# A dense layer's norm: from per-token sums and diagonal matrices to column-strip sums and transfers, its steps begun earlier

## The chip, the core and the metric

The kernel runs on one core of a Trainium2 chip. What is measured is the device time of one execution, in microseconds (us). The core has five engines that run side by side, each taking its own instructions in the order in which the program issued them: TensorE (PE, with its weight loads PEld), VectorE (DVE), ScalarE (ACT), GpSimd (POOL) and SyncE (SP), which issues the DMA transfers. Engines wait for each other through semaphores only.

## What is computed

Three layers, one after the other, on 2 x 768 = 1536 tokens of width 512. Layer 1 is attention with 8 heads of 64, masked to keys whose 6-bit hash bucket is that of the query. Layer 2 is a dense gated layer that begins with a root-mean-square norm of each token, and layer 3 sends each token to one of 8 experts. The change touches the norm of layer 2 alone:

```
def _moe_ref(x, w_gate, w_val, w_out, rms_g):
    rms = np.sqrt(np.mean(x * x, axis=-1, keepdims=True) + 1e-06)
    xn = x / rms * rms_g
    g = xn @ w_gate
    silu = g * (1.0 / (1.0 + np.exp(-g)))
    val = xn @ w_val
    return (silu * val @ w_out).astype(np.float32)
```

## The kernel before

Activations lie transposed: features on the 128 partitions (four chunks of 128, `NK`), tokens along the free dimension, in three blocks of 512 tokens (`xyt[0]` to `xyt[2]`). A norm needs, for every token, a sum over features, which means over partitions and chunks, and then the root's inverse on every partition again. `xnorm(b)` returns the steps of that for block `b`:

- `square` (twice, on ACT): squares of two chunks each, 128x1024, into `xf`.
- `add` (three times, on DVE): the four squared chunks are added to one.
- `mean`: on PE, four products whose loaded weights are the 128 columns of squares and whose moving operand is one column of ones. The sums come out one token per partition, in PSUM (128x4). DVE scales them into `r`, POOL raises them to the power -1/2.
- `spill`, `flat`, `diag` (eight times), all on POOL: the 128x4 roots are split into a high and a low part, a tile of ones is written, and eight 128x128 diagonal matrices are made of the parts.
- `spread`: on PE, two products (128x512) of the tile of ones with the diagonals, so that every partition holds every token's root; ACT copies that to `rb`.
- `scale`, `high`, `low` (four times each): the normed chunks and their high and low parts in `RG`, which PE reads.

The order of the work is written out by hand. In `attention()` every step is put into a list with a position, `at(pos, step)`, and the list is issued in the order of the positions. One unit of attention (128 queries of one head) has 1000 positions, and there are 96 units. The unit's steps are `qk` (scores into one of two PSUM halves, L530 and L532), `stats` (DVE, row maximum, L545 and L546), `expo` (ACT, L559; the half is free again after it), `scales` (POOL, L554), `back` (PE transposes, L568, into one of three banks that `psH()` hands out in turn), `emptied` (copies of those, L572, on ACT or DVE) and, every four units, the product with the values (L589) and its copy (L599). The norm of block 0 stands at the positions of `PLAN["xn"]`.

In `moe1()` the dense layer runs in 36 steps `n`, 12 for each block. A step issues, in this order: the high and low parts of the weights of step n+1 (`split`, L317 on ACT, L318 on DVE or POOL), the gate and value products of step n (24 products of 128x512, L345 to L347) with their activation (ACT L750, DVE L751 and L752, ACT L754 for the high part `hh`), then what `win[n]` holds, with a PSUM half as argument, then what `cal[n]` holds, then `h_low(n)` (DVE L759) and the products `down(n-1)` (12 of 128x512, L770 to L772). Weights of the second half of this layer arrive as 64-bit floats and are converted on DVE and ACT in `cal[0]` to `cal[9]` (L244, L248, L252 and L792). The norms of blocks 1 and 2 are put into `win` and `cal` from step `o` on, which is step 0 for block 1 and step 13 for block 2:

```
            for f_ in win.pop(n, ()):
                f_(psA(True))
```

`psA(True)` is the PSUM half that the gate products of step n+1 write next. SP issues all transfers of this stretch: the rows of q, k and their hash bits to other partitions (L490, L493, L496, L514), loads (L238, L395, L403), and the result of a block (L778).

Of the kernel before, what the change touches and what calls it, by code (L numbers as in the profile page):

```python
# [15 lines left out]
P = 128  # L16
# [29 lines left out]
    "cv": (-4, 3532, 7612, 8983, 10967),  # L46
    "late": 2000,
    "v": 11280,
    "xn": ((59501, 60423), (62683, 62816, 63235), 64180, 61519, 64439, (71025, 67128, 68518, 70395), 72597, (74588, 92089, 73653, 83058), (86240, 93654, 83020, 84060), (89992, 93958, 86081, 95569)),
    "splits": ((-6894, 1, 0, 0), (-10825, 1, 0, 1), (-4899, 0, 0), (1381, 1, 1, 0), (8244, 1, 1, 1)),  # L50
    "ahead": ((215, 2), (3057, 4), (4742, 6), (17871, 8)),
    "batches": (2, 2, 3, 2, 3, 2, 3, 2, 3, 2),
# [27 lines left out]
def tile_kernel(  # L80
# [51 lines left out]
    def f32(ap):  # L132
        return ap.bitcast(F32)
# [16 lines left out]
    def rg(off, n, parts=P):  # L150
        return RG[0:parts, off : off + n]
# [108 lines left out]
    def xnorm(b):  # L260

        xf = ch4(BB[:, 0:2048])
        rb = EX[:, 1536:2048]
        at_ = X_AT[b] if b else 17 * S
        dg = [rg(at_ + y * 512, 512).rearrange("p (t q) -> p t q", t=TPB) for y in range(2)]
        st = {}

        def square(hf):
            sl = slice(2 * hf, 2 * hf + 2)
            nc.scalar.activation(out=xf[:, sl], in_=xyt[b][:, sl], func=AF.Square)  # L270

        def add(x):
            i, j = ((0, 2), (1, 3), (0, 1))[x]
            TT(out=xf[:, i], in0=xf[:, i], in1=xf[:, j], op=ALU.add)

        def mean(ps):
            for t in range(TPB):
                mm(ps[:, t : t + 1], lhsT=xf[:, 0, t * P : (t + 1) * P], rhs=ones[:, 0:1], start=True, stop=True)
            r = st["r"] = sp.tile([P, 2 * TPB], F32, tag="r", name="r", bufs=2)
            TS(r[:, 0:TPB], ps[:, 0:TPB], 1.0 / DM, 1e-6, ALU.mult, ALU.add)  # L280
            PTT(out=r[:, TPB:], in0=r[:, 0:TPB], in1=half, op=ALU.pow)

        def spill():
            r = st["r"]
            rr = st["rr"] = sp.tile([P, 2 * TPB], F32R, tag="rr", name="rr", bufs=2)
            copyP(out=rr[:, 0:TPB], in_=r[:, TPB:])
            PTT(out=rr[:, TPB:], in0=r[:, TPB:], in1=f32(rr[:, 0:TPB]), op=ALU.subtract)

        def flat():
            copyP(out=rg(at_ + 1024, P), in_=ones)  # L290

        def diag(z):
            PTS(dg[z // TPB][:, z % TPB], ident, f32(st["rr"][:, z : z + 1]), 1.0, ALU.mult, ALU.mult)

        def spread(ps):
            for y in range(2):
                mm(ps[:, 0:TB], lhsT=rg(at_ + 1024, P), rhs=dg[y].rearrange("p t q -> p (t q)"), start=(y == 0), stop=(y == 1))
            copyA(out=rb, in_=ps[:, 0:TB])

        def scale(k):  # L300
            STT(out=xf[:, k], in0=xyt[b][:, k], scalar=gcol[:, k : k + 1], in1=rb, op0=ALU.mult, op1=ALU.mult)

        def high(k):
            copyA(out=xpart(b, 0, k), in_=xf[:, k])

        def low(k):
            (PTT if b else TT)(out=xpart(b, 1, k), in0=xf[:, k], in1=f32(xpart(b, 0, k)), op=ALU.subtract)

        return dict(square=square, add=add, mean=mean, spill=spill, flat=flat, diag=diag, spread=spread, scale=scale, high=high, low=low)


    GV_AT = (4096, 10240)
# [366 lines left out]
    def attention():  # L679
        start_up()  # L680
        for u in range(NU):
            for name, f in (("qk", qk), ("exp", expo), ("tr", back), ("stats", stats)):
                at(PLAN["first"][name].get(u, 1000 * u + PLAN[name][u % 4]), f, u)
            for hf in range(2):
                at(PLAN["first"]["copy"].get(2 * u + hf, 1000 * u + PLAN["copy"][u % 4][hf]), emptied, u, hf)
        for u in range(0, NU, 2):
            at(PLAN["first"]["scales"].get(u, 1000 * u + PLAN["scales"][u // 2 % 2]), scales, u)
        for g in range(NU // 4):
            av_steps(g)
        for p in range(1, NPAIR):  # L690
            cast, low, q_rows, k_rows, ql_rows, bits, signs, place = prep(p)
            o = (p - 1) * PER * 1000 + (PLAN["late"] if p == 1 else 0)

            def put(name, f, *a):
                at(PLAN["first"]["pair"].get(name, o + PLAN[name]) if p == 1 else o + PLAN[name], f, *a)

            for j in range(2):
                put(f"cast{j}", cast, j)
                put(f"low{j}", low, j)
            put("q_rows", q_rows)  # L700
            put("k_rows", k_rows)
            put("ql_rows", ql_rows)
            put("bits", bits)
            put("signs", signs)
            put("place", place, 0)
            put("place2", place, 1)
            if p + 2 < NPAIR:
                put("load", load, p + 2)
            at((p - 1) * PER * 1000 + PLAN["v"], load_v, p)
        for x in range(12):  # L710
            for y, f in enumerate((cv_load, cv_rebias, cv_shift, cv_low, cv_sign)):
                at(max(6000 * x + PLAN["cv"][y], PLAN["ramp"]["cv"]), f, x)
        for x in range(12, 15):
            at(1000 * (NU - 9) + 500, cv_load, x)
        xn = xnorm(0)
        sq, ad, me, fl, sp_, dg, sd, sc, hi_, lo_ = PLAN["xn"]
        for x in range(2):
            at(sq[x], xn["square"], x)
        for x in range(3):
            at(ad[x], xn["add"], x)  # L720
        at(me, lambda: xn["mean"](psH()))
        at(fl, xn["flat"])
        at(sp_, xn["spill"])
        for z in range(2 * TPB):
            at(dg[z // 2], xn["diag"], z)
        at(sd, lambda: xn["spread"](psH()))
        for k in range(NK):
            at(sc[k], xn["scale"], k)
            at(hi_[k], xn["high"], k)
            at(lo_[k], xn["low"], k)  # L730
        for x_, f, *a in PLAN["splits"]:
            at(1000 * NU + x_, split_gv if f else split_o, *a)
        for x_, z in PLAN["ahead"]:
            at(1000 * NU + x_, gate_products, 0, 0, z)
        for _, _, f, a in sorted(cal, key=lambda z: z[:2]):
            f(*a)


    def moe1(rt):
# [57 lines left out]
        for b in range(1, NBLK):  # L797
            xn = xnorm(b)
            o = (b - 1) * NF + (0 if b == 1 else 1)
            cal[o].append(lambda f=xn["square"]: f(0))  # L800
            cal[o + 1].append(lambda f=xn["square"]: f(1))
            for x in range(3):
                cal[o + 2 + x].append(lambda f=xn["add"], x=x: f(x))
            win[o + 6].append(lambda ps, xn=xn: (xn["mean"](ps), xn["spill"](), xn["flat"](), [xn["diag"](z) for z in range(2 * TPB)]))
            win[o + 7].append(xn["spread"])
            for k in range(NK):
                cal[o + 8 + k // 2].append(lambda xn=xn, k=k: (xn["scale"](k), xn["high"](k)))
                cal[o + 9 + k // 2].append(lambda f=xn["low"], k=k: f(k))
# [637 lines left out]
```

## Time and profile before

| | |
|---|---|
| median of 3 runs | 651.41 us (650.35 to 651.6) |
| the profiled execution: its own time | 652.19 us |
| the profiled execution: span of its instructions | 650.4 us |
| mean granted TensorE clock | 0.995 |
| busy, of the span: PE, PEld, DVE, ACT, POOL | 98%, 78%, 81%, 62%, 43% |
| instructions | 10537 |

The execution's own time is 1.8 us longer than the span, which is what lies before the first and after the last instruction. Attention takes the span to about 237 us, the dense layer to about 532 us, the experts the rest. A busy share is an average over the span; what a change is worth is read from its own stretch, and from what the engine that never rests there waits for. In rows of the order of time, an `x8` is eight instructions in one row, and `[0.81 <-PE PS L568]` is idle time of the engine just before, with what ended it.

### The profile page before, as it was taken

How to read it: one execution, taken by the hardware profiler on the slowest of the kernel's cores; microseconds unless marked ns; L12 is line 12 of the kernel's file. 1: busy time of each engine (PE TensorE's matmuls, PEld its weight loads, DVE VectorE, ACT ScalarE, POOL GpSimd, SP SyncE). 2: the span in 40 equal slices, each digit the busy share in tenths (PEclk: the TensorE clock that was granted, in tenths of full speed). 3: DMA queues.
4: the chain of work that ended last, by engine and by line, in shares of the span. 5: the costliest groups of instructions: out<-in, count | busy, mean ns of one | idle time of the engine just before them, and what ended most of it. 6: DMA issues, size and time to landing. Idle time of an engine off the chain costs nothing. (4 is left out here: it accounts for less than half of the span.)

```text
span 650.4 us, 10537 instructions
## 1 busy us (share of the span) xinstructions
PE 638.1 (98%) x3604; PEld 508.7 (78%) x3605; DVE 529.7 (81%) x907; ACT 401.6 (62%) x726; POOL 280.6 (43%) x329
## 2 busy tenths in 40 slices
PE   8999999999999999999999999999999999999996
PEld 5776777777777778887888888888888888888884
DVE  6787878889887839998966786799999476999994
ACT  6687888888889847555444333343334253888782
POOL 4676566768866603563622215431123425111211
PEclk9999999999999999999999999999999999999998
DMA  7637447364243204551301000002405015999930
GB/s 228 166 94 204 119 129 186 101 201 126 88 106 124 66 33 142 192 183 67 126 20 65 1 2 0 1 1 103 161 6 189 0 71 166 384 390 390 389 131 26
DMA packets 43399, 84.16 MB, mean 129 GB/s; under 512 B 3500, under 2 KB 17020, under 8 KB 43216
## 3 DMA queue, kind: packets, MB, share of 16 engines
q1 hardware_dynamic: 41840, 80.17, 38.2%
q0 software_dynamic: 1360, 3.20, 1.4%
q8 instruction: 29, 0.48, 0.3%
q14 instruction: 26, 0.21, 0.1%
q10 hardware_dynamic: 144, 0.10, 0.1%
HBM read 67.16 MB, written 5.24 MB: 111 GB/s over the span
## 5 line engine op out<-in xcount | busy, mean ns | idle before, releaser
L318 POOL TENSOR_TENSOR RG<-WW,RG 128x512 fp32r<-128x512 f32 x35 | 65.0, 1857 | 177.8 <-ACT RG L317 170.1
L345 PE MATMUL PS<-RG 128*128 128x512 f32 x288 | 112.5, 391 | 0.0
L346 PE MATMUL PS<-RG 128*128 128x512 f32 x288 | 112.1, 389 | 0.0
L347 PE MATMUL PS<-RG 128*128 128x512 f32 x288 | 112.1, 389 | 0.0
L545 DVE TENSOR_REDUCE peak<-PS 128x1 f32<-128x768 f32 x96 | 91.6, 954 | 21.9 <-PE PS L532 15.0
L559 ACT ACTIVATE WW<-PS,shape 128x768 f32<-128x768 f32 x96 | 95.4, 999 | 10.2 <-DVE shape L546 9.2
L554 POOL TENSOR_SCALAR WW<-WW,rsum 128x768 f32<-128x768 f32 x96 | 87.3, 922 | 4.8
L754 ACT CAST RG<-BB 128x512 fp32r<-128x512 f32 x36 | 22.4, 621 | 107.7 <-DVE BB L752 107.7
L568 PE MATMUL PS<-cst,WW 128*128 128x128 f32 x576 | 81.3, 277 | 1.6 <-POOL WW L554 1.6
L568 PEld LDWEIGHTS PS<-cst,WW 128*128 128x128 f32 x576 | 64.1, 140 | 21.4 <-POOL WW L554 12.6
L1119 DVE TENSOR_TENSOR RG<-WW,RG 128x1024 fp32r<-128x1024 f32 x64 | 75.3, 1220 | 5.9 <-ACT RG L1117 4.1
L318 DVE TENSOR_TENSOR RG<-WW,RG 128x512 fp32r<-128x512 f32 x73 | 61.0, 873 | 8.3 <-ACT RG L317 8.3
L317 ACT CAST RG<-WW 128x512 fp32r<-128x512 f32 x108 | 61.4, 617 | 8.1 <-PE PS L772 4.2
L1117 ACT CAST RG<-WW 128x1024 fp32r<-128x1024 f32 x64 | 63.9, 1052 | 1.2 <-PE PS L1174 0.9
L345 PEld LDWEIGHTS PS<-RG 128*128 128x128 f32 x288 | 54.1, 188 | 11.8 <-issue 0.8
L347 PEld LDWEIGHTS PS<-RG 128*128 128x128 f32 x288 | 54.1, 188 | 11.3
L346 PEld LDWEIGHTS PS<-RG 128*128 128x128 f32 x288 | 54.1, 188 | 11.1
L770 PE MATMUL PS<-RG 128*128 128x512 f32 x144 | 56.5, 392 | 0.0
L772 PE MATMUL PS<-RG 128*128 128x512 f32 x144 | 56.3, 391 | 0.1
L771 PE MATMUL PS<-RG 128*128 128x512 f32 x144 | 56.0, 389 | 0.0
L530 PE MATMUL PS<-RG 128*128 128x512 f32 x192 | 55.5, 370 | 0.2 <-ACT WW L559 0.2
L907 DVE CUSTOM_DVE_ANT_0 EX<-XY,SS 128x512 f32<-128x512 f32 x64 | 50.1, 782 | 1.6
(207 smaller groups left out, 1263.1 us busy)
## 6 DMA issues: line engine op xcount, KB each, us to landing
WW<-in_w SPq DMA_DIRECT2D x32, 1024.0 KB
RG<-RG SPq DMA_DIRECT2D x28, 384.0 KB
WW<-in_kq SPq DMA_DIRECT2D x7, 768.0 KB
SS<-in_wo SPq DMA_DIRECT2D x9, 512.0 KB
SS<-in_wg SPq DMA_DIRECT2D x8, 512.0 KB
SS<-in_wv SPq DMA_DIRECT2D x8, 512.0 KB
WW<-in_v SPq DMA_DIRECT2D x8, 384.0 KB
XY<-in_wg SPq DMA_DIRECT2D x4, 512.0 KB
```

The source lines that it names most:

```text
L317: copyA(out=hi, in_=src)
L318: sub(out=lo, in0=src, in1=f32(hi), op=ALU.subtract)
L345: mm(o, lhsT=h[:, k], rhs=xpart(b, 0, k), start=(k == 0), stop=False)
L346: mm(o, lhsT=h[:, k], rhs=xpart(b, 1, k), start=False, stop=False)
L347: mm(o, lhsT=l[:, k], rhs=xpart(b, 0, k), start=False, stop=(k == NK - 1))
L545: red(out=a[:, 1:2], in_=u_st[u][:, 0:S], axis=AX.X, op=ALU.max, negate=True)
L554: PTS(e_t(x), e_t(x), rsum[:, x % NS : x % NS + 1], 1.0, ALU.mult, ALU.mult)
L559: nc.scalar.activation(out=e_t(u), in_=s[:, 0:S], func=AF.Exp, bias=c, scale=b, accum_out=sums[:, u % NS : u % NS + 1])
L568: nc.tensor.transpose(ps[:, x * P : (x + 1) * P], e_t(u)[:, kt * P : (kt + 1) * P], ident)
L770: mm(acc[t], lhsT=hh[:, sl], rhs=oh, start=(f == 0), stop=False)
L1117: copyA(out=hi[:, sl], in_=src[:, sl])
L1119: f(out=lo[:, sl], in0=src[:, sl], in1=f32(hi[:, sl]), op=ALU.subtract)
```

## The change

The tokens' sums are formed by another product. The loaded weights are now 32 columns of ones and the moving operand is the 128 columns of squares, once for each of the block's four token groups, each into a strip of 32 partitions of the same 128 PSUM columns. ACT copies that 128x128 strip picture to `sq` (in `rb`'s place), and four transfers take one partition's row of 128 sums of each strip to one column of `r`, a token per partition. `root` is the former scaling (now from SBUF) and power. `lay` is a transfer of the 128x4 roots to a row of the output tensor in HBM (its last, which is written with its real values later), and `spread` is a transfer of that row to all 128 partitions of `rb`. The tile of ones, the two parts, the eight diagonals, the two products and the copy of them are gone.

The steps also stand elsewhere. Block 0: squares, additions and mean five units earlier, the root and the rest where `PLAN["xn"]` now says; `scale`, `high` and `low` where they stood. Blocks 1 and 2: the second square in step o (was o+1), the additions in o+1 and o+2 (were o+2 to o+4), the mean in o+3 (was o+6), root and `lay` in o+5, `spread` in o+6 (its former products in o+7).

```
--- before.py
+++ after.py
@@ -46,7 +46,7 @@
     "cv": (-4, 3532, 7612, 8983, 10967),
     "late": 2000,
     "v": 11280,
-    "xn": ((59501, 60423), (62683, 62816, 63235), 64180, 61519, 64439, (71025, 67128, 68518, 70395), 72597, (74588, 92089, 73653, 83058), (86240, 93654, 83020, 84060), (89992, 93958, 86081, 95569)),
+    "xn": ((54501, 55423), (57683, 57816, 58235), 59180, 62000, 62950, 67500, (74588, 92089, 73653, 83058), (86240, 93654, 83020, 84060), (89992, 93958, 86081, 95569)),
     "splits": ((-6894, 1, 0, 0), (-10825, 1, 0, 1), (-4899, 0, 0), (1381, 1, 1, 0), (8244, 1, 1, 1)),
     "ahead": ((215, 2), (3057, 4), (4742, 6), (17871, 8)),
     "batches": (2, 2, 3, 2, 3, 2, 3, 2, 3, 2),
@@ -261,8 +261,8 @@
 
         xf = ch4(BB[:, 0:2048])
         rb = EX[:, 1536:2048]
-        at_ = X_AT[b] if b else 17 * S
-        dg = [rg(at_ + y * 512, 512).rearrange("p (t q) -> p t q", t=TPB) for y in range(2)]
+        sq = rb[:, 0:P]
+        line = out[NT - 1 : NT, :]
         st = {}
 
         def square(hf):
@@ -275,27 +275,22 @@
 
         def mean(ps):
             for t in range(TPB):
-                mm(ps[:, t : t + 1], lhsT=xf[:, 0, t * P : (t + 1) * P], rhs=ones[:, 0:1], start=True, stop=True)
+                mm(ps[32 * t : 32 * t + 32, 0:P], lhsT=ones[:, 0:32], rhs=xf[:, 0, t * P : (t + 1) * P], start=True, stop=True)
+            copyA(out=sq, in_=ps[:, 0:P])
             r = st["r"] = sp.tile([P, 2 * TPB], F32, tag="r", name="r", bufs=2)
-            TS(r[:, 0:TPB], ps[:, 0:TPB], 1.0 / DM, 1e-6, ALU.mult, ALU.add)
+            for t in range(TPB):
+                dma(out=r[:, t : t + 1], in_=sq[32 * t : 32 * t + 1, :])
+
+        def root():
+            r = st["r"]
+            TS(r[:, 0:TPB], r[:, 0:TPB], 1.0 / DM, 1e-6, ALU.mult, ALU.add)
             PTT(out=r[:, TPB:], in0=r[:, 0:TPB], in1=half, op=ALU.pow)
 
-        def spill():
-            r = st["r"]
-            rr = st["rr"] = sp.tile([P, 2 * TPB], F32R, tag="rr", name="rr", bufs=2)
-            copyP(out=rr[:, 0:TPB], in_=r[:, TPB:])
-            PTT(out=rr[:, TPB:], in0=r[:, TPB:], in1=f32(rr[:, 0:TPB]), op=ALU.subtract)
-
-        def flat():
-            copyP(out=rg(at_ + 1024, P), in_=ones)
-
-        def diag(z):
-            PTS(dg[z // TPB][:, z % TPB], ident, f32(st["rr"][:, z : z + 1]), 1.0, ALU.mult, ALU.mult)
-
-        def spread(ps):
-            for y in range(2):
-                mm(ps[:, 0:TB], lhsT=rg(at_ + 1024, P), rhs=dg[y].rearrange("p t q -> p (t q)"), start=(y == 0), stop=(y == 1))
-            copyA(out=rb, in_=ps[:, 0:TB])
+        def lay():
+            dma(out=line.rearrange("o (t p) -> p (o t)", p=P), in_=st["r"][:, TPB:])
+
+        def spread():
+            dma(out=rb, in_=line.broadcast_to([P, TB]))
 
         def scale(k):
             STT(out=xf[:, k], in0=xyt[b][:, k], scalar=gcol[:, k : k + 1], in1=rb, op0=ALU.mult, op1=ALU.mult)
@@ -306,7 +301,7 @@
         def low(k):
             (PTT if b else TT)(out=xpart(b, 1, k), in0=xf[:, k], in1=f32(xpart(b, 0, k)), op=ALU.subtract)
 
-        return dict(square=square, add=add, mean=mean, spill=spill, flat=flat, diag=diag, spread=spread, scale=scale, high=high, low=low)
+        return dict(square=square, add=add, mean=mean, root=root, lay=lay, spread=spread, scale=scale, high=high, low=low)
 
 
     GV_AT = (4096, 10240)
@@ -713,17 +708,15 @@
         for x in range(12, 15):
             at(1000 * (NU - 9) + 500, cv_load, x)
         xn = xnorm(0)
-        sq, ad, me, fl, sp_, dg, sd, sc, hi_, lo_ = PLAN["xn"]
+        sq, ad, me, ro, ly, sd, sc, hi_, lo_ = PLAN["xn"]
         for x in range(2):
             at(sq[x], xn["square"], x)
         for x in range(3):
             at(ad[x], xn["add"], x)
         at(me, lambda: xn["mean"](psH()))
-        at(fl, xn["flat"])
-        at(sp_, xn["spill"])
-        for z in range(2 * TPB):
-            at(dg[z // 2], xn["diag"], z)
-        at(sd, lambda: xn["spread"](psH()))
+        at(ro, xn["root"])
+        at(ly, xn["lay"])
+        at(sd, xn["spread"])
         for k in range(NK):
             at(sc[k], xn["scale"], k)
             at(hi_[k], xn["high"], k)
@@ -797,12 +790,14 @@
         for b in range(1, NBLK):
             xn = xnorm(b)
             o = (b - 1) * NF + (0 if b == 1 else 1)
-            cal[o].append(lambda f=xn["square"]: f(0))
-            cal[o + 1].append(lambda f=xn["square"]: f(1))
+            for x in range(2):
+                cal[o].append(lambda f=xn["square"], x=x: f(x))
             for x in range(3):
-                cal[o + 2 + x].append(lambda f=xn["add"], x=x: f(x))
-            win[o + 6].append(lambda ps, xn=xn: (xn["mean"](ps), xn["spill"](), xn["flat"](), [xn["diag"](z) for z in range(2 * TPB)]))
-            win[o + 7].append(xn["spread"])
+                cal[o + 1 + x // 2].append(lambda f=xn["add"], x=x: f(x))
+            win[o + 3].append(xn["mean"])
+            cal[o + 5].append(xn["root"])
+            cal[o + 5].append(xn["lay"])
+            cal[o + 6].append(xn["spread"])
             for k in range(NK):
                 cal[o + 8 + k // 2].append(lambda xn=xn, k=k: (xn["scale"](k), xn["high"](k)))
                 cal[o + 9 + k // 2].append(lambda f=xn["low"], k=k: f(k))
```

Four places where instructions move. The changed file is five lines shorter from the norm on and seven lines shorter from the dense layer on, so that L572, L559 and L599 of before are L567, L554 and L594 there, and L751, L754, L759, L318 and L792 are L744, L747, L752, L313 and L785.

ACT in attention, about 132 us into the span; before:

```order
L559 ACTIVATE WW,sums<-PS,shape 128x768 x2
L572 COPY WW<-PS 128x3x128 x4
L559 ACTIVATE WW,sums<-PS,shape 128x768 x2
L572 COPY EX<-PS 128x3x128
L599 COPY XY<-PS 128x256
L572 COPY BB<-PS 128x3x128 x2
L559 ACTIVATE WW,sums<-PS,shape 128x768 x2
L572 COPY EX<-PS 128x3x128
L270 ACTIVATE BB<-XY 128x1024
```

and of the change:

```order
L554 ACTIVATE WW,sums<-PS,shape 128x768 x2
L567 COPY WW<-PS 128x3x128 x2
L270 ACTIVATE BB<-XY 128x1024 x2
L567 COPY WW<-PS 128x3x128 x2
L554 ACTIVATE WW,sums<-PS,shape 128x768 x2
L567 COPY EX<-PS 128x3x128
L594 COPY XY<-PS 128x256
L567 COPY BB<-PS 128x3x128 x2
L554 ACTIVATE WW,sums<-PS,shape 128x768 x2
L567 COPY EX<-PS 128x3x128
```

Both squares of block 0 stand now one after the other between two pairs of copies and ahead of two exponentials; before, they stood apart and two groups of exponentials later. The copy of the sums (L279) is new.

DVE in attention, about 139 us; before, and then of the change:

```order
L546 SCALAR_TENSOR_TENSOR shape<-PS,peak 128x2
L248 SCALAR_TENSOR_TENSOR WW<-SS,WW 128x512
L572 COPY EX<-PS 128x3x128
L252 SCALAR_TENSOR_TENSOR WW<-SS,WW 128x512
L545 TENSOR_REDUCE peak<-PS 128x1
L546 SCALAR_TENSOR_TENSOR shape<-PS,peak 128x2
```

```order
L541 SCALAR_TENSOR_TENSOR shape<-PS,peak 128x2
L248 SCALAR_TENSOR_TENSOR WW<-SS,WW 128x512
L274 TENSOR_TENSOR BB<-BB 128x512 x3
L567 COPY EX<-PS 128x3x128
L252 SCALAR_TENSOR_TENSOR WW<-SS,WW 128x512
L540 TENSOR_REDUCE peak<-PS 128x1
L541 SCALAR_TENSOR_TENSOR shape<-PS,peak 128x2
```

All three additions stand ahead of a copy out of PSUM and of the row maximum of the next unit.

DVE in step 1 of the dense layer (the row of two L318 is the split for step 2); before:

```order
L318 TENSOR_TENSOR RG<-WW,RG 128x512 x2
L751 SCALAR_TENSOR_TENSOR BB<-BB,PS 128x512
L752 SCALAR_TENSOR_TENSOR BB<-BB,PS 128x512
L244 TENSOR_SCALAR WW<-EX 128x512
L244 TENSOR_SCALAR WW<-EX 128x4x128
L248 SCALAR_TENSOR_TENSOR WW<-SS,WW 128x512
L248 SCALAR_TENSOR_TENSOR WW<-XY,WW 128x4x128
L252 SCALAR_TENSOR_TENSOR WW<-EX,WW 128x512
L252 SCALAR_TENSOR_TENSOR WW<-EX,WW 128x4x128
L759 TENSOR_TENSOR RG<-BB,RG 128x512
```

and of the change:

```order
L313 TENSOR_TENSOR RG<-WW,RG 128x512 x2
L744 SCALAR_TENSOR_TENSOR BB<-BB,PS 128x512
L745 SCALAR_TENSOR_TENSOR BB<-BB,PS 128x512
L274 TENSOR_TENSOR BB<-BB 128x512 x2
L244 TENSOR_SCALAR WW<-EX 128x512
L244 TENSOR_SCALAR WW<-EX 128x4x128
L248 SCALAR_TENSOR_TENSOR WW<-SS,WW 128x512
L248 SCALAR_TENSOR_TENSOR WW<-XY,WW 128x4x128
L252 SCALAR_TENSOR_TENSOR WW<-EX,WW 128x512
L252 SCALAR_TENSOR_TENSOR WW<-EX,WW 128x4x128
L752 TENSOR_TENSOR RG<-BB,RG 128x512
```

Two additions stand ahead of the conversion's six instructions and of `h_low` (L759, now L752), which follows them.

ACT in step 3 of the dense layer; before:

```order
L317 CAST RG<-WW 128x512 x3
L750 ACTIVATE BB<-PS 128x512
L754 CAST RG<-BB 128x512
L792 ACTIVATE EX<-XY 128x512 x2
L792 ACTIVATE BB<-WW 128x512
```

and of the change:

```order
L312 CAST RG<-WW 128x512 x3
L743 ACTIVATE BB<-PS 128x512
L747 CAST RG<-BB 128x512
L279 COPY EX<-PS 128x128
L785 ACTIVATE EX<-XY 128x512 x2
L785 ACTIVATE BB<-WW 128x512
```

The copy of the sums' strips follows the cast of `hh` (L754, now L747) of that step.

## Rows read from the trace of the kernel before

**Rows 1.** The page: busy us of each engine, share of the span, instructions.
```profile
PE 638.1 (98%) x3604; PEld 508.7 (78%) x3605; DVE 529.7 (81%) x907; ACT 401.6 (62%) x726; POOL 280.6 (43%) x329
```

**Rows 2.** In order of time, PE in attention: start us, us, engine, line, operation.
```profile
154.86 0.95 PE L278 MATMUL PS<-ones,BB 128*128 128x1 f32 x8
155.67 0.85 PE L568 MATMUL PS<-cst,WW 128*128 128x128 f32 x6
...
174.31 0.63 PE L297 MATMUL PS<-RG 128*128 128x512 f32 x2
174.88 0.85 PE L505 MATMUL PS<-WW,padg 128*32 128x384 f32 x8
```

**Rows 3.** In order of time, PE in the dense layer, blocks 1 and 2.
```profile
294.69 0.39 PE L297 MATMUL PS<-RG 128*128 128x512 f32 x1
...
295.72 0.40 PE L770 MATMUL PS<-RG 128*128 128x512 f32 x1
...
403.20 0.62 PE L297 MATMUL PS<-RG 128*128 128x512 f32 x2
403.65 0.39 PE L770 MATMUL PS<-RG 128*128 128x512 f32 x1
```

**Rows 4.** In order of time, PE after the dense layer: products into 32-partition strips.
```profile
534.56 0.64 PE L927 MATMUL PS<-BB,EX 128*32 128x128 f32 x16
```

**Rows 5.** In order of time, ACT in attention, 132 to 142 us.
```profile
132.14 0.85 ACT L572 COPY WW<-PS 128x384 f32<-128x384 f32 x2
133.81 0.86 ACT L572 COPY WW<-PS 128x384 f32<-128x384 f32 x2 [0.81 <-PE PS L568]
134.55 1.01 ACT L559 ACTIVATE WW<-PS,shape 128x768 f32<-128x768 f32 x1
...
141.13 1.07 ACT L270 ACTIVATE BB<-XY 128x1024 f32<-128x1024 f32 x1
```

**Rows 6.** In order of time, PE in attention: two score products.
```profile
136.05 0.59 PE L530 MATMUL PS<-RG 128*128 128x512 f32 x2
...
144.67 0.59 PE L530 MATMUL PS<-RG 128*128 128x512 f32 x2
```

**Rows 7.** In order of time, DVE in attention: a row maximum, and two additions.
```profile
141.45 0.95 DVE L545 TENSOR_REDUCE peak<-PS 128x1 f32<-128x768 f32 x1
...
149.27 1.28 DVE L274 TENSOR_TENSOR BB<-BB 128x512 f32<-128x512 f32 x2
```

**Rows 8.** In order of time, DVE in steps 1 to 3 of the dense layer.
```profile
251.66 0.69 DVE L759 TENSOR_TENSOR RG<-BB,RG 128x512 fp32r<-128x512 f32 x1
...
254.06 0.69 DVE L751 SCALAR_TENSOR_TENSOR BB<-BB,PS 128x512 f32<-128x512 f32 x1 [0.24 <-ACT BB L750]
...
263.27 0.69 DVE L752 SCALAR_TENSOR_TENSOR BB<-BB,PS 128x512 f32<-128x512 f32 x1
```

**Rows 9.** PE in order of time: third product of `down(1)`, of `down(2)`; first of step 4.
```profile
253.05 0.39 PE L772 MATMUL PS<-RG 128*128 128x512 f32 x1
...
261.42 0.50 PE L772 MATMUL PS<-RG 128*128 128x512 f32 x1
...
263.82 0.39 PE L345 MATMUL PS<-RG 128*128 128x512 f32 x1
```

**Rows 10.** In order of time, ACT: the cast of step 3; a later copy of 128x128.
```profile
263.99 0.62 ACT L754 CAST RG<-BB 128x512 fp32r<-128x512 f32 x1 [4.60 <-DVE BB L752]
...
535.05 0.27 ACT L928 COPY EX<-PS 128x128 f32<-128x128 f32 x1 [0.23 <-PE PS L927]
```

**Rows 11.** SP: four transfers in order of time; who waited for whom (us, times, longest).
```profile
149.37 3.19 SPq L514 DMA_DIRECT2D RG<-RG  x4
...
SPq L514 <- DMA RG<-RG: 12.9, 7, 3.5
```

**Rows 12.** Busy us by stretch: length, PE (instructions), PEld, DVE, ACT, POOL, PEclk, DMA, GB/s.
```profile
253.00:261.10 8.10, 8.10 (x37) 6.58 (x36) 7.75 (x15) 4.84 (x10) 3.48 (x2) 1.00 0.38 128
345.00:353.00 8.00, 8.00 (x37) 6.64 (x36) 5.20 (x11) 3.73 (x6) 1.80 (x1) 1.00 0.00 0
```

## The prediction

> **What bounds the kernel now.** I read the busy shares first: PE is at work for 98% of the span [rows 1], and no other engine comes near. The stretches of the two layers in which the norms stand say the same, PE busy for all of 8.10 and 8.00 us [rows 12]. So an instruction taken off PE there is worth its own time, and a wait of PE costs its own time; it has no rest in which to make one up. The second thing to see is who stands close behind PE. In the dense layer's first steps, where DVE also converts weights, DVE is busy 7.75 of 8.10 us; in the steps of block 2 it is busy 5.20 of 8.00 us [rows 12]. A DVE or ACT step that moves is therefore free in block 2 and can be dear in block 1. The rows in order of time then give the prices.
>
> **What leaves PE.** The mean of before takes PE from 154.86 to 155.67 us, 0.81 us [rows 2]; the other two means read the same: 3 x 0.81 = 2.43 us. The spread takes 0.57 us in block 0 (174.31 to 174.88) [rows 2], 1.03 us in block 1 (294.69 to 295.72, with a wait for POOL's diagonals between its two products) and 0.45 us in block 2 [rows 3]: 2.05 us. Together 4.48 us. What leaves POOL (ones, parts, 24 diagonals) I cost at nothing beyond that wait: PE waits there for nothing else of POOL's.
>
> **What comes to PE.** Four products into four 32-partition strips, which this trace has not in this place. From below, the same form elsewhere: 16 records in 0.64 us [rows 4], so 0.32 us for 8. From above, the strip products of 384 columns, 8 records in 0.85 us [rows 2]. The columns are 128, so it is nearest the first; with the change of form around it I take 0.4 us for a block.
>
> **Block 0, the squares.** Between two pairs of copies ACT rests for 0.81 us (until 133.81); both squares, 1.07 us each, now go there [rows 5]. 2.14 - 0.81 = 1.33 us, less some 0.15 us by which neighbours overlap (1.07 us each is the whole of one, and ACT starts the next before its end): 1.2 us late for the exponential at 134.55. It ended at 135.56 [rows 5], and PE's scores at 136.05 need the PSUM half that it reads [rows 6]: 0.49 us of slack. PE waits 1.2 - 0.49 = 0.7 us.
>
> **Block 0, the additions.** Three additions of 0.64 us (1.28 us for two) now stand ahead of the row maximum at 141.45 [rows 7]. It is 1.9 us late from that and 0.7 us from PE's own delay, 2.6 us. Maximum and exponential (0.95 + 1.01 us) ended by 143.4 at the earliest [rows 5, 7], and an estimated 0.2 us later with the small instruction between them, 143.6; PE wanted the half at 144.67 [rows 6], and now, late by 0.7 and by the mean's 0.4 us, at 145.8. 143.6 + 2.6 = 146.2: PE waits 0.4 us, or 0.5 with its restart. Block 0 adds 0.7 + 0.4 + 0.5 = 1.6 us. That DVE and ACT are freed of these steps where they stood gives nothing, for PE did not wait for them there.
>
> **Block 1.** First `h_low(1)`: it ended at 252.35 [rows 8], and the third product of `down(1)` read it at 253.05 [rows 9]. The second square on ACT (about 0.2 us of it reaches DVE) and two additions (1.2 us in a stream) now come before it: ready at 253.75, 0.7 us too late, and 0.1 us for PE to restart, as at 261.42, where before had the same wait [rows 9]. Then the new copy. The sums lie in the PSUM half that the gate products of step 4 write, so those wait for ACT's copy, which stands behind the cast of step 3, which waits for DVE. DVE, 1.4 us late, makes up about 0.6 us in the small gaps that it had before its next products (0.24 us is one of them [rows 8]), so its last product at 263.27 [rows 8] moves to 264.1 and ends at 264.8; cast 0.62 and copy 0.27 us [rows 10]: 265.7 us. The gate products of step 4 began at 263.82 [rows 9]. PE is 1.9 us behind, and that holds the waits and the mean itself, whose 0.4 us pass inside. The moved third addition gives DVE its time back only after that.
>
> **Block 2.** DVE rests for 2.8 of 8 us [rows 12], and the cast there comes with DVE not behind, so the copy is done before the next step. Only the mean's 0.4 us.
>
> **The transfers.** I cost them at nothing, because of time that covers them. In block 0 the sums lie in SBUF at about 144.0 us (the additions end late, at 143.4, the mean and the copy follow). Four transfers at 3.19 / 4 = 0.8 us each [rows 11] are issued by 147.2. The root stands where two additions stood, at 149.27 [rows 7], with PE's delay at 150.8. The longest that SP ever waited for such a transfer to land is 3.5 us [rows 11]: 150.7, just in time. Past that point DVE stands, and behind it the maxima, the exponentials and PE. The row of roots has four and a half units (a unit is (144.67 - 136.05) / 4 = 2.2 us [rows 6]) before `spread`; it goes ahead of the four placements that started at 149.37 [rows 11], which serve scores some 20 us later, and waits on POOL's power, which is short. In blocks 1 and 2 whole steps lie between. The Trainium skill, "DMA: Bandwidth & Descriptors", section "Rules for kernel authors", speaks against such transfers: a strided last dimension becomes one descriptor per element, and many small transfers are mostly overhead. By the fixed 2.0 us of its section on the anatomy of a DMA they would still land by 149.2 us and the sum would stay; by the row's 3.5 us it stays too, with 0.1 us to spare.
>
> **Sum.** -4.48 + 1.6 + 1.9 + 0.4 = -0.6 us: the profiled execution's 652.19 becomes 651.6. It lies 0.8 us above the median of the runs, so against that, 651.41 - 0.6 = **650.8 us**. A measurement of this kernel tells about 0.2% (1.3 us) from no change; this is no change that it can tell.
>
> **Rivals.**
> - *The new waits don't form.* My slacks are differences of a few tenths, read from rows in which engines hand work on with overlaps. If ACT and DVE absorb the moved steps, only PE's own time counts: -4.48 + 3 x 0.32 = -3.5 us, 647.9 us. For it: no engine but PE is above 81% [rows 1]. Against it: DVE's 7.75 of 8.10 us [rows 12], and the wait at 261.42 that stands in the rows already. Chance 0.28.
> - *The four small transfers come late, and it is slower.* If they are served one after the other, each with the 3.5 us of rows 11, the last lands at 144.0 + 14 = 158.0, 7.2 us after the root's place; less the 1.0 us between 143.6 and 144.67, PE waits 6.2 us: 657.0 us. It decides from about 4.6 us between the last issue and its landing. For it: each has 128 runs of 4 bytes, and no row shows such a transfer. Against it: SP's queue does not wait for one before it issues the next. By the page's 2.0 us each it would be 0.2 us, 651.0 us. Chance 0.08.
> - *The strips don't run abreast*, so that the change doesn't do what it says: the mean costs 0.8 us as before, 0.4 us more in blocks 0 and 2 (in block 1 it passes in the wait): 651.6 us. The 16 records in 0.64 us speak against it [rows 4]. Chance 0.06.
>
> **How the numbers follow.** My forecast has 0.58. Its own bounds: without the waits of block 0, 649.6; with no slack anywhere (0.8 + 0.85 + 1.9 us in block 0, 2.6 in block 1, 0.85 in block 2), 654. Most of it, 0.40, lies within 0.2%, 0.10 faster, 0.08 slower. With the rivals: faster 0.10 + 0.28 = 0.38; same 0.40 + 0.06 + 0.02 = 0.48; slower 0.08 + 0.06 = 0.14. The range reaches down to the first rival and up to 653.2, which leaves out the late transfers and the last part of the upper bound. The forecast alone: 649.6 to 652.8.
>
> **What would show it.** Right: three means of about 0.4 us; PE waiting for ACT's exponential near 136 us and again near 146; in the dense layer a wait for `h_low` in `down(1)` and one for the new copy ahead of step 4; step 8 beginning where it did. Wrong: none of these waits and a span 3 us shorter; or DVE's small instruction on `r` waiting for a transfer; or `scale` waiting for `rb`, which would mean that the way through HBM takes longer than ten microseconds.

## The result, and the profile after

The changed kernel takes 660.17 us (median of 6 runs, 658.47 to 663.09); the kernel before, on the same chip, 651.5 us (6 runs). The ratio is 1.0137, 95% interval 1.0113 to 1.0161: some 9 us slower, outside the predicted range. The profiled execution is the slowest of the six: 663.09 us with a span of 661.3.

PE's share of the span [rows 1] now reads:

```profile
PE 640.5 (97%) x3598; PEld 508.8 (77%) x3599; DVE 530.9 (80%) x907; ACT 400.8 (61%) x726; POOL 262.9 (40%) x296
```

To find the place I took the same products of PE in both traces and noted by how much later each starts in the changed kernel. What passes before 50 us differs from execution to execution (by 1.77 us here), so only differences from stretch to stretch count. Beside it stand the prediction's terms and three experiments told below (e4: the early steps alone; f3: block 0 as before; f4: 512 small stores alone).

| What PE loses in the stretch, us | predicted | change | e4 | f3 | f4 |
|---|---|---|---|---|---|
| block 0, squares (to 136.1) | +0.7 | +0.63 | +0.62 | 0 | 0 |
| block 0, additions and product (to 152) | +0.9 | +1.91 | +3.62 | 0 | 0 |
| block 0, old product gone (156) | -0.81 | -0.85 | -0.84 | 0 | 0 |
| block 0, old spread gone; **the stop** (170 to 184) | -0.57 | **+7.15** | +0.04 | 0 | **+7.70** |
| block 1, squares to product (to 280) | +1.9 | +1.93 | +1.52 | +1.95 | 0 |
| block 1, old product and spread gone (to 310) | -1.84 | -2.04 | -1.29 | -2.04 | 0 |
| block 1, last steps (to 340) | 0 | +0.41 | 0 | +1.72 | 0 |
| block 2 | -0.86 | -0.83 | 0 | -0.83 | 0 |

(Times at left are those of before. e4 keeps the old product, 0.8 us, and moves it; why its additions cost some 0.9 us more than the change's beyond that is not traced. The last steps of block 1 cost 1.5 to 1.6 us in e1, e2 and e3 too. A last 0.8 us of the change's profiled run, near 550, is in no other run.) One line makes the result. The stretch in question, by windows, first of before, then of the change (columns: us, then busy us with the number of instructions for PE, PEld, DVE, ACT, POOL, then PEclk, DMA share, GB/s):

```profile
154.00:162.00 8.00, 8.00 (x63) 6.46 (x63) 7.08 (x13) 5.99 (x15) 7.28 (x11) 1.00 0.88 227
174.00:180.00 6.00, 6.00 (x48) 3.94 (x46) 5.78 (x10) 5.08 (x11) 4.54 (x6) 1.00 0.02 6
180.00:190.00 10.00, 10.00 (x77) 7.31 (x76) 8.91 (x16) 8.71 (x19) 7.13 (x10) 1.00 0.60 125
```

```profile
154.00:162.00 8.00, 8.00 (x61) 5.99 (x59) 6.80 (x12) 7.17 (x15) 7.45 (x10) 1.00 0.10 12
162.00:174.00 12.00, 12.00 (x90) 9.43 (x90) 10.82 (x19) 9.39 (x21) 6.32 (x9) 1.00 0.93 219
174.00:180.00 6.00, 1.34 (x12) 0.70 (x8) 0.71 (x2) 3.31 (x7) 2.77 (x5) 0.93 0.30 94
180.00:190.00 10.00, 10.00 (x56) 7.39 (x56) 6.92 (x12) 4.66 (x9) 5.36 (x8) 0.70 0.12 47
```

From 154 to 162 us before moves 227 GB/s; the change moves 12, and makes up for it until 174. Then PE stands, 1.34 of 6 us busy, and for the next ten its granted clock is 0.70 of full speed: 56 products instead of 77 in the same busy time (0.50 from 180 to 184, the lower of the clock's two levels, and 1.00 again from 187). The transfers were late first; PE stops at 175.07, some 20 us after them. SP's issues, POOL and PE in order of time show the way from one to the other (start, duration; in brackets the idle time before and what ended it). First the load of the weight piece and its use by POOL before, then the change:

```profile
162.04 0.55 SPq L238 DMA_DIRECT2D SS<-in_wo  x1
...
168.26 0.65 POOL L241 TENSOR_SCALAR SS<-SS 128x512 f32<-128x512 f32 x1
```

```profile
149.30 0.39 SPq L238 DMA_DIRECT2D SS<-in_wv  x1
155.41 0.39 SPq L290 DMA_DIRECT2D out<-r  x1
155.90 5.28 SPq L509 DMA_DIRECT2D RG<-RG  x4
161.28 2.64 SPq L485 DMA_DIRECT2D RG<-RG  x2
163.98 0.60 SPq L390 DMA_DIRECT2D WW<-in_kq  x1
...
167.16 0.59 SPq L488 DMA_DIRECT2D RG<-RG  x1
167.80 0.59 SPq L238 DMA_DIRECT2D SS<-in_wo  x1
```

```profile
154.00 1.38 POOL L287 TENSOR_TENSOR r<-r,half 128x4 f32<-128x4 f32 x1 [1.02 <-DVE r L286]
...
176.96 0.65 POOL L241 TENSOR_SCALAR SS<-SS 128x512 f32<-128x512 f32 x1 [6.42 <-DMA SS<-in_wo]
```

```profile
172.81 0.82 PE L563 MATMUL PS<-cst,WW 128*128 128x128 f32 x6
...
179.73 1.54 PE L563 MATMUL PS<-cst,WW 128*128 128x128 f32 x6 [4.66 <-POOL WW L549]
```

`lay` (L290) is issued at 155.41. The four placements behind it take 5.28 us to issue where they took 3.19 [rows 11], the next two 2.64. Of the four, one alone takes 2.72 us, though nothing that it waits for is late. The load of the dense layer's weight piece goes out at 167.80 and lands at 176.81. POOL meets that piece's conversion (L241) in its own order, ahead of the scaling that attention needs (L549), and stands 6.42 us; PE waits for the scaling, and its next six products take 1.54 us instead of 0.82. Two suspects are in these rows: SP itself, which stood from 149.69 to 155.41 until POOL's power (ended 155.38) let it issue `lay`, and what `lay` did after that. PE is 4.30 us late itself there, start-up included, so the placements, which started at 149.37 before [rows 11], are 2.2 us later than PE's own lateness explains (155.90 - 149.37 - 4.30).

### The profile page after: what moved, and what is told of

It is laid out like the page before. It is cut to its first block, busy times and chain, and to the rows that moved or that the text cites. A ratio compares the mean times of both kernels' runs of the same rounds, so it can differ in the third digit from the quotient of the medians.

```text
span 661.3 us, 10508 instructions
## 1 busy us (share of the span) xinstructions
PE 640.5 (97%) x3598; PEld 508.8 (77%) x3599; DVE 530.9 (80%) x907; ACT 400.8 (61%) x726; POOL 262.9 (40%) x296
## 5 line engine op out<-in xcount | busy, mean ns | idle before, releaser
L313 POOL TENSOR_TENSOR RG<-WW,RG 128x512 fp32r<-128x512 f32 x35 | 64.1, 1833 | 192.4 <-ACT RG L312 188.7
L554 ACT ACTIVATE WW<-PS,shape 128x768 f32<-128x768 f32 x96 | 95.3, 997 | 12.7 <-DVE shape L541 11.4
L563 PE MATMUL PS<-cst,WW 128*128 128x128 f32 x576 | 83.2, 281 | 6.3 <-POOL WW L549 6.2
L549 POOL TENSOR_SCALAR WW<-WW,rsum 128x768 f32<-128x768 f32 x96 | 87.2, 920 | 4.8
L747 ACT CAST RG<-BB 128x512 fp32r<-128x512 f32 x36 | 22.4, 622 | 105.2 <-DVE BB L745 105.2
L563 PEld LDWEIGHTS PS<-cst,WW 128*128 128x128 f32 x576 | 65.8, 143 | 26.3 <-POOL WW L549 16.1
L313 DVE TENSOR_TENSOR RG<-WW,RG 128x512 fp32r<-128x512 f32 x73 | 61.8, 883 | 10.7 <-ACT RG L312 10.7
L527 PE MATMUL PS<-RG 76*128 76x512 f32 x192 | 50.8, 346 | 2.1 <-ACT WW L554 2.1
```

The lines of the kernel that those rows point to most:

```text
L313: sub(out=lo, in0=src, in1=f32(hi), op=ALU.subtract)
L549: PTS(e_t(x), e_t(x), rsum[:, x % NS : x % NS + 1], 1.0, ALU.mult, ALU.mult)
L554: nc.scalar.activation(out=e_t(u), in_=s[:, 0:S], func=AF.Exp, bias=c, scale=b, accum_out=sums[:, u % NS : u % NS + 1])
L563: nc.tensor.transpose(ps[:, x * P : (x + 1) * P], e_t(u)[:, kt * P : (kt + 1) * P], ident)
```

## The experiments

Three theories. **Wait**: SP stands for POOL's power, and all behind is late. **Pieces**: the 512 pieces of 4 bytes of `lay` hold the transfers. **Steps**: the early squares, additions and products.

**e1, `lay` behind the load** (block 0 only).

```diff
-    "xn": (..., 59180, 62000, 62950, 67500, ...
+    "xn": (..., 59180, 62000, 65998, 67500, ...
```

> Block 0's transfer of the roots (`lay`) goes behind the load of the dense layer's weight piece instead of ahead of four placements; nothing else differs from the change. The queue theory (what stands behind `lay` on SP comes late: the placements, the load of the piece, POOL's in-order conversion, the scaling, PE): the load is issued by 166, POOL's 6.4 us wait and PE's 4.7 us wait near 179 us go, PEclk stays at 1.00 there, and the time is 651 to 653 us against 660.2 of the change. The steps theory (the squares, additions and sums that now come early cost it): 658 us or more, the PE stop stays.

Measured 658.06 us, ratio 1.0085 (1.0052 to 1.0118). The load goes out at 162.82, and POOL and the scaling no longer wait for it (POOL rests 0.82 us before the conversion, for DVE). But PE still loses 3.6 us in this stretch, to what now stands behind `lay`:

```profile
162.82 1.39 SPq L238 DMA_DIRECT2D SS<-in_wo  x1
164.30 1.43 SPq L290 DMA_DIRECT2D out<-r  x1
165.82 3.15 SPq L509 DMA_DIRECT2D RG<-RG  x4
176.03 0.34 SPq L293 DMA_DIRECT2D EX<-out  x1
```

```profile
176.44 0.59 PE L527 MATMUL PS<-RG 76*128 76x512 f32 x2 [2.26 <-DMA RG<-RG]
```

The placements hold PE for 2.26 us, and `spread` (L293), which waits for `lay` to land, goes out 11.7 us after it. The trouble moved with `lay`. So the queue theory (wait or pieces) holds, but its number (651 to 653) fell, and by the number alone the steps theory (658 or more) was met: I had taken the place behind the load to be free.

**e2, the roots of one partition early, the others late.**

```diff
...
-        at(ly, xn["lay"])
+        at(ly, xn["lay"], 0, 1)
+        at(65998, xn["lay"], 1, P)
```

Here `lay` takes a range of partitions as arguments.

> As the run with `lay` behind the load, but the roots of partition 0 (4 pieces of 4 bytes) are still stored at the change's place, so SP waits for POOL's power there as in the change, and only 508 of 512 pieces go later. If SP's wait makes the loss (wait theory): 657 to 660 us, the placements start at 155.9 and POOL still waits for the piece. If the 512 pieces in the DMA rings make it (pieces theory): 651 to 654 us, the four placements take 3.2 us instead of 5.3, the two after them 1.4 instead of 2.6, and the load comes early enough. Steps theory: 658 or more.

Measured 665.1 us, ratio 1.0202 (1.0155 to 1.0249). The total answers neither theory, since the 508 late pieces did more harm than 512 in e1: the four placements behind them took 12.13 us to issue and PE waited 6.84 us for them. Why 127 partitions are worse than 128 the trace shows in part: the packets of the 508 pieces pass about two at a time, from 169.23 to 177.81 us, while f4's 512 pass up to 19 at a time within 0.8 us. One of the four placements takes 9.80 us to issue in that time. The early part does answer: SP stood for the power until 152.01, as in the change by PE's clock (152.01 - 0.92 against 155.41 - 4.30), and the placements then took 3.25 us. The load went out at 162.62, only 0.5 us later than before once PE's own offset of 0.08 us is taken off. But what stood ahead of it in the queue was later, and POOL waits for it, although most of its packets were through before the 508 pieces' began:

```profile
170.61 0.66 POOL L241 TENSOR_SCALAR SS<-SS 128x512 f32<-128x512 f32 x1 [3.45 <-DMA SS<-in_wo]
```

```profile
173.40 0.88 PE L563 MATMUL PS<-cst,WW 128*128 128x128 f32 x6 [1.71 <-POOL WW L549]
```

In e1, without the wait, neither of these stops is there. So the wait, with four pieces, already stops PE for 1.71 us where the change stops it for 4.66. The wait theory holds for a part; no run has the wait without any piece.

**e3, 128 runs of 16 bytes instead of 512 of 4**, at the change's place.

```diff
-            dma(out=line.rearrange("o (t p) -> p (o t)", p=P), in_=st["r"][:, TPB:])
+            dma(out=line.rearrange("o (p t) -> p (o t)", t=TPB), in_=st["r"][:, TPB:])
...
```

> `lay` stays where the change has it, but stores each partition's four roots as one run of 16 bytes (128 runs instead of 512), in all three blocks; the scaling reads the row in that order. Pieces theory: the placements take about 3.2 and 1.4 us instead of 5.3 and 2.6, the load comes some 3 us earlier, PE's stop shrinks from 4.7 to under 2 us, and the time is 652 to 656 us. Wait theory: no change, 658 to 661 us. Steps theory: 658 to 661 us.

Measured 658.77 us, ratio 1.0114 (1.0061 to 1.0166). The total misses the 652 to 656 of the pieces theory and meets the two others, but its four runs reach from 657.01 to 663.14, and the profiled one took 657.2. In its trace PE's stop is 2.52 us instead of 4.66, and the stretch costs 4.19 us instead of 7.15. Over the 1.71 us of e2, 128 pieces add 0.81 us to the stop and 512 add 2.95, about as their numbers (an estimate, if wait and pieces add up). Clearer is block 1, where nothing else is near. Windows behind `lay` there, first of the change (512 pieces, issued at 292.16), then of e3 (128 runs, issued at 285.80):

```profile
295.00:303.00 8.00, 8.00 (x37) 6.63 (x36) 7.18 (x13) 1.81 (x3) 1.36 (x1) 1.00 0.40 27
303.00:306.00 3.00, 3.00 (x15) 2.49 (x14) 1.23 (x3) 0.82 (x2) 0.00 (x0) 1.00 1.00 299
```

```profile
287.50:289.50 2.00, 2.00 (x11) 1.65 (x10) 1.94 (x4) 1.10 (x3) 1.03 (x1) 1.00 0.23 39
289.50:293.00 3.50, 3.50 (x17) 2.92 (x16) 1.73 (x4) 0.72 (x2) 1.10 (x1) 1.00 1.05 340
```

Two weight loads were queued behind `lay` each time. They crawl at 27 GB/s for 8 us behind 512 pieces, at 39 GB/s for 2 us behind 128, then run at some 300. By these windows that is 16 ns a piece in both (8 / 512, 2 / 128), but the loads' own start is in them. In before, the same two loads reach their full rate 1.9 us after the first issue; in the change they take 10.9 us, in e3 3.2. That leaves 9.0 us for 512 pieces and 1.4 for 128, some 18 and 11 ns a piece (estimates from the traces' packets). Whether the size counts too is not settled.

**e4, the early steps alone**: before's norm, its squares, additions and product at the change's places.

> The kernel before with the squares, the additions and the product for the mean at the change's earlier places, in all blocks; the mean in its old form, the diagonals and the spread by PE where they stood, no small transfers. Steps theory: 658 to 661 us, as the change. Queue theories: the early steps cost what the change's trace shows of them, 0.6 for the squares and 1.5 for the additions in block 0 and 1.8 in block 1, of which some comes back: 652 to 655 us.

Measured 655.74 us, ratio 1.0059 (1.0039 to 1.0079): 3.3 us over before, 0.7 above the range that the queue theories gave and 2.3 below that of the steps theory. The steps theory falls as the cause of the 9 us; the steps have a price, and the table shows where.

**f1, the roots taken on the strips**, so that no small piece is left.

```diff
-            TS(r[:, 0:TPB], r[:, 0:TPB], 1.0 / DM, 1e-6, ALU.mult, ALU.add)
-            PTT(out=r[:, TPB:], in0=r[:, 0:TPB], in1=half, op=ALU.pow)
+            TS(sq, sq, 1.0 / DM, 1e-6, ALU.mult, ALU.add)
+            PTT(out=sq, in0=sq, in1=half, op=ALU.pow)
...
```

The four transfers to `r` go too, and `lay` stores four strips' rows in 4 runs of 512 bytes.

> The change with the roots taken on the strips as they lie (128 x 128 instead of 128 x 4), so that no transfer of 4-byte pieces is left: the four `r` transfers go, and `lay` stores 4 runs of 512 bytes at the change's place. If the pieces written to HBM hold the transfers (pieces theory): the placements behind `lay` take 3.2 and 1.4 us, POOL waits for no load, PE does not stop near 175 us, and what is left is the early steps against the products removed: block 0 +1.1, block 1 -0.1, its last steps +0.4 to +1.5, block 2 -0.8, so 0.6 to 1.7 us over the kernel before. If SP's wait for POOL's power makes the loss (wait theory), or the early steps do: 6 us or more over it, as in the change.

Measured 696.1 us. It says nothing of the theories, for POOL's power had another price than I took for granted:

```profile
150.75 21.17 POOL L283 TENSOR_TENSOR EX<-EX,half 128x128 f32<-128x128 f32 x1 [1.08 <-DVE EX L282]
```

128 elements a partition take 21.17 us, 4 took 1.38 in the change. The same form with the steps where before has them (f2) took 695.17 us, for the same reason.

**f3, block 0 as before, blocks 1 and 2 as in the change.**

> Block 0's norm as in the kernel before, steps and form; blocks 1 and 2 as in the change, with their transfers of 4-byte pieces. If all of the loss is made in block 0 (pieces and wait theories; in blocks 1 and 2 the loads have steps to spare): block 1 -0.1, its last steps +0.4 to +1.5, block 2 -0.8, so 0.5 us under to 0.6 us over the kernel before. If the transfers cost in every block: 3 us or more over it.

Measured 652.34 us, ratio 1.0002 (0.998 to 1.0024). As far as 0.2% can tell, all of the loss is block 0's. `lay` lands late in blocks 1 and 2 too (10.2 and 8.8 us after its issue), but there PE loses nothing to it.

**f4, the suspect alone**: the kernel before and one store.

```diff
         at(me, lambda: xn["mean"](psH()))
+        at(63001, lambda: dma(out=out[NT - 1 : NT, :].rearrange("o (t p) -> p (o t)", p=P), in_=gcol))
```

> The kernel before, with one thing added: a store of a 128 x 4 constant to the same 2 KB row of HBM in 512 pieces of 4 bytes, issued on SP in block 0 behind the four placements (some 2.5 us later in SP's order than the change's `lay`); nothing waits for its data, and SP waits for nothing new. Pieces theory: no other transfer moves at more than some 30 GB/s for about 8 us, the pair of placements, the load of the keys and the load of the piece come some 5 to 8 us later, and PE loses 2 to 8 us. Wait theory and steps theory: within 1 us of the kernel before.

Measured 660.96 us, ratio 1.0118 (1.0082 to 1.0155): the change's loss, with nothing else of the change. The store stands behind the four placements, and SP waits for no power. SP waits at L493 instead, 5.5 us, until the two placements right behind the store have landed. From the load on, which goes out at 168.55, the chain is the change's:

```profile
176.06 0.64 POOL L241 TENSOR_SCALAR SS<-SS 128x512 f32<-128x512 f32 x1 [5.54 <-DMA SS<-in_wo]
```

```profile
178.83 1.54 PE L568 MATMUL PS<-cst,WW 128*128 128x128 f32 x6 [4.97 <-POOL WW L554]
```

PE loses 7.70 us at the place where the change loses 7.15 (7.72 without the old spread, 0.57, that went).

**g1, the same store with each piece in a row of its own; g2, the same 2 KB in 4 runs.**

```diff
+        at(63001, lambda: dma(out=out[0:TB, 0:1].rearrange("(t p) o -> p (t o)", p=P), in_=gcol))
```

> The kernel before with the same added store of 512 pieces of 4 bytes at the same place, but each piece goes to another 2 KB row of the output instead of all into one row. If each small write to HBM has its own price: as with one row, 6 to 9 us over the kernel before, and some 8 us in which other transfers crawl. If it is the one row that all pieces meet in (they wait for one another there): within 1 us of the kernel before.

> The kernel before with a store of the same 2 KB to the same row at the same place on SP, in 4 runs of 512 bytes instead of 512 of 4. Pieces theory: within 1 us of the kernel before. If any store there, or the one place more in SP's queue, makes the loss: 5 us or more over it.

Measured 652.17 us, ratio 1.0 (0.9979 to 1.0022), and 651.3 us, 1.0001 (0.9976 to 1.0026). 512 pieces of 4 bytes cost nothing if they go to 512 rows. The windows behind the store, first of f4, then of g1:

```profile
157.50:161.50 4.00, 4.00 (x34) 3.04 (x34) 3.30 (x7) 2.77 (x7) 3.77 (x5) 1.00 1.26 78
172.00:178.00 6.00, 1.85 (x16) 0.94 (x14) 1.45 (x4) 3.91 (x8) 1.67 (x4) 0.98 0.68 166
```

```profile
157.50:161.50 4.00, 4.00 (x34) 3.04 (x34) 3.32 (x7) 2.79 (x6) 3.72 (x5) 1.00 0.99 245
172.00:178.00 6.00, 6.00 (x47) 4.00 (x47) 5.21 (x11) 5.26 (x12) 5.63 (x11) 1.00 0.01 3
```

In both the DMA engines count as fully busy (share 1.26 and 0.99), but in f4 they move 78 GB/s, in g1 245. So it is not the count of pieces alone, nor their size, but that all of them end in one 2 KB row. The store lands 11.6 us after its issue in f4, 1.9 in g1 and 1.7 in g2. The traces' packets add where the time goes: the pieces' own packets take 9 ns at most and are through by 156.3 us in f4 and g1, but afterwards packets of other transfers stand, single ones of 3072 bytes for up to 5.1 us in f4 (0.23 as a rule, under 0.6 us always in g1).

The landing of the weight piece sets the parts side by side. By PE's clock (each run's lateness of PE at 160 us taken off) it lands later than before by 1.0 us in e1, 3.7 in e2, 4.5 in e3, 6.7 in the change, 7.0 in f4 and 0.9 in g1. So the wait (e2) is a large part of the change's lateness, and f4's pieces make as much without it.

**g3, h1, a version without such pieces.** The roots go back within SBUF to four rows and from there in 4 runs of 512 bytes; blocks 0 and 2, squares and additions where before has them; block 1 as before. h1 is g3 with two of block 0's scalings back near their place in before. Part of the edit of both:

```diff
         def lay():
-            dma(out=line.rearrange("o (t p) -> p (o t)", p=P), in_=st["r"][:, TPB:])
+            for t in range(TPB):
+                dma(out=sq[32 * t : 32 * t + 1, :], in_=st["r"][:, TPB + t : TPB + t + 1])
+
+        def row():
+            dma(out=line.rearrange("o (t p) -> (o t) p", p=P), in_=sq[0:P:32, :])
...
```

> Blocks 0 and 2 with the sums on strips and the spread by transfers, but the roots go back within SBUF to four rows (4 transfers of 128 pieces of 4 bytes) and from there to HBM in 4 runs of 512 bytes; squares, additions and product where the kernel before has them (block 2's product one step earlier), block 0's transfers behind the keys' load and behind the second placements. Block 1 as before. Pieces theory, with 4-byte pieces within SBUF harmless: block 0 -1.0 us, block 2 -0.9 us, about 2 us under the kernel before. If pieces of 4 bytes hold the transfers wherever they go: 5 us or more over it.

> As g3, with block 0's first two scalings back beside DVE's move of the bits, where the kernel before has them. In g3 PE lost 0.9 us near 188 us to an exponential that waited behind one of the two. If that wait was theirs, it goes: block 0 at -0.8 us, block 2 at -0.8 us, 1.6 us under the kernel before (ratio 0.9975). If the row comes too late for the scaling (its broadcast was issued at 173.3 and the scaling then wants it at 177), DVE waits and PE loses 0.5 us or more.

g3: 651.46 us, ratio 0.9981 (0.9959 to 1.0003), not clear of the kernel before and short of the 2 us expected: PE lost 0.9 us near 188 to an exponential. h1: 650.52 us, ratio 0.997 (0.9951 to 0.9988), by 0.3% faster than the kernel before, and without that loss. In h1 PE gains 0.83 us in block 0 (its product takes 0.43 us, the old spread is gone) and 0.82 in block 2. The way through SBUF is short (issues of SP):

```profile
167.12 2.48 SPq L345 DMA_DIRECT2D EX<-r  x4
171.17 0.59 SPq L348 DMA_DIRECT2D out<-EX  x1
172.88 0.33 SPq L351 DMA_DIRECT2D EX<-out  x1
```

The last of these waits for the store to land: 1.7 us after its issue, where it was 11.7 in e1. g3 and h1 also leave the early steps out, so no run has the change's steps without its pieces.

## Why the prediction was wrong

**The step that failed is "The transfers. I cost them at nothing, because of time that covers them."** The stop that they made measured +7.7 us. I looked for the danger at the four `r` transfers, and those were in time: the last landed at 150.01, and DVE took the root at 153.77 without waiting for them. Of `lay` I wrote that it "goes ahead of the four placements that started at 149.37, which serve scores some 20 us later". That looked at the placements, which were early enough, and not at the rest of SP's queue: the load of the weight piece, which comes behind five further issues, had to land by 168.26, when POOL's conversion began in before without a wait. That `lay` "waits on POOL's power, which is short" took the power's length (1.38 us) for SP's wait, which was 5.7 us. And I priced a store of 512 pieces by its own landing, not by what it does to the transfers behind it. f4 shows that price, g1 its condition: all pieces in one row. How the wait and the pieces share the change's 7.7 us is not settled: f4 has the whole of it without the wait, and e2 has 1.71 us of PE's stop with hardly a piece.

The Trainium skill, "DMA: Bandwidth & Descriptors", section "Why small descriptors are slow (HBM only)", says that transfers within SBUF don't suffer from small descriptors and puts the slowness to HBM down to overheads of each descriptor. The first agrees with the runs: g3 and h1 have 4-byte pieces within SBUF, and in h1 PE gains 0.83 us in that block. The second does not give this price: by it g1 would be as slow as f4, and g1's ratio is 1.0. The 2.0 us that the prediction took from the same page stand there for transfers that GpSimd issues; the trace agrees for the four `r` transfers, which SP issues: each landed 2.0 to 2.1 us after its issue, the last at 150.01.

**The rival with the late transfers** had the right sign and about the right size (657.0 us), but for the wrong transfers and without the others behind them. That its size came near is luck.

**Right, by the table:** "What leaves PE" and the product on strips, for which I took 0.4 us:

```profile
145.29 0.42 PE L278 MATMUL PS<-BB,ones 128*32 128x128 f32 x8 [0.86 <-DVE BB L274]
```

"Block 0, the squares" (0.7; 0.63 measured), "Block 1" (1.9; 1.93) with the wait for the new copy ahead of step 4, and "Block 2".

```profile
264.40 0.50 PE L765 MATMUL PS<-RG 128*128 128x512 f32 x1 [0.58 <-DVE RG L752]
276.23 0.50 PE L340 MATMUL PS<-RG 128*128 128x512 f32 x1 [0.51 <-ACT EX L279]
```

**Too small: "Block 0, the additions"**, 0.9 us with the product, 1.91 measured. The additions took 0.82 us each (2.46 for three), not 0.64, and the product itself waits for them 0.86 us in PE's order; I had counted only the maxima behind them.

**Missing: the last steps of block 1.** What PE gains there it waits for DVE later: 0.41 us in the change, 1.72 in f3, where PE's waits for `h_low` (L806) over the whole run read:

```profile
PE PS L819 <- DVE RG L806: 2.1, 3, 1.1
```

Two of the three, 1.5 us, fall between 300 and 345, where before has none. DVE is nearly full there in before:

```profile
320.00:330.00 10.00, 9.91 (x44) 7.86 (x43) 9.79 (x12) 4.24 (x8) 6.44 (x6) 1.00 0.57 238
```

I should have asked who sets the pace once PE has less to do. That DVE's load is the reason is read from rows; no run took work off DVE there, and why the change lost only 0.41 is open.

Without the stop the change would by the table have come out some 0.6 to 1.9 us over before, not 0.6 under it (an estimate): -0.6, with 1.0 more for the additions and 0.4 to 1.7 for DVE, less 0.2 for block 1's old products.

**Open:** why one row holds all transfers (whether it is the 2 KB row, or a smaller or larger unit), why e2's pieces pass so few at a time, and the share of SP's wait.

## What to carry to other kernels

Price a transfer by what it does to those queued behind it, count the wait of the queue for its data, and follow that queue to the first load with a due time, even if that load serves another layer: an engine that converts it in order passes the delay on. Turn a column of small results into a row within SBUF and write the row in long runs; do not let hundreds of small pieces meet in one row of HBM. And where a second engine is nearly full, time taken off the first is only lent.

## What the runs showed of the hardware

- Stores of 4 or 16 bytes into one 2 KB row of HBM held other transfers for some 18 and 11 ns each (estimates: 9.0 us for 512 in the change, 1.4 for 128 in e3), though their own packets took 9 ns at most; 512 of 4 bytes into 512 rows cost nothing that could be measured (ratio 1.0, 0.9979 to 1.0022).
- POOL's power took 21.17 us for 128 elements a partition (f1), 1.38 us for 4 (the change).
- After PE's stop of 4.66 us the granted clock over ten us was 0.70, so the products at the lower of the two levels made up some 3 of the 7.7 us (an estimate: 7.7 - 4.66; f4: 7.70 - 4.97 = 2.7).
